# Attention with a compressive memory, mixed with a gated MLP: the memory update on four column groups, placed behind a visit's logits

## The chip, the cores and the metric

The kernel runs on one core of a Trainium2 chip. A core has a matrix engine (TensorE, "PE", with its weight loads shown apart as "PEld"), three engines for element-wise work (VectorE "DVE", ScalarE "ACT", GpSimd "POOL"), a queue for transfers (SyncE "SP"), and two memories: SBUF, 128 partitions, and PSUM, into which PE alone writes its products. The metric is the device time of one execution in microseconds, as the median of several runs. Profiles are of one more execution.

## What is computed

Cut from the reference; B = 1, S = 2048 tokens, D = 512, 32 heads of 16 channels, 4 segments of L = 512 tokens, MLP width 1792. All inputs are bf16.

```python
g = sigmoid((x * gate_w).sum(-1))                 # a gate for each token
return g * A(x) + (1 - g) * B(x)

def B(x):                                         # gated MLP
    return (gelu(x @ w_gate) * (x @ w_up)) @ w_down

def A(x):                                         # attention by segments, with a memory
    q, k, v = x @ wq, x @ wk, x @ wv              # as (head, segment, L, 16)
    phi = lambda t: where(t > 0, t + 1, exp(t))
    M, z = 0, 0                                   # for each head 16 x 16, and 16
    for s in range(4):
        p = softmax(qs @ ks.T * 16 ** -0.5 + causal_mask)
        a_dot = p @ vs
        a_mem = (phi(qs) @ M) / (phi(qs) @ z + 1e-6)
        o = sigmoid(beta) * a_mem + (1 - sigmoid(beta)) * a_dot
        M = M + phi(ks).T @ vs
        z = z + phi(ks).sum(over tokens)
    return concat(o) @ wo
```

The memory update of the last two lines of the loop is what the change is about. It is needed after segments 0, 1 and 2.

## The kernel before

Channels lie on partitions and tokens in the free dimension for q and k: four blocks `c` of 128 channels, which are eight heads each. Scores are computed transposed, 64 keys at a time, with the softmax left unnormalized (no row maximum; a bound on the logits that is computed on the way decides at the end whether a slow general branch has to redo the work, which these inputs don't need).

**Visits.** The work around the change is ordered by hand, when the program is built, by a loop over 72 *visits* (lines 991 to 1034), 18 for each segment (`NP`). A visit issues the logits of one or two key blocks (`group_qk`, line 643: matmuls of 32 rows by 128 columns of the array, the four heads of one parity in four row groups), one exponential over four PSUM banks on ACT, and causal selects on POOL. Two visits after the last block of a channel block follows its `lump`: 64 products of the probabilities with V (`pv`, line 663, arrays of 64 rows by 32 columns, tile `od`), their transposes on DVE (`oq`), normalization and transposes back over the next visits. `clock[0]` counts visits.

**Fill.** Between visits PE works on units from several streams: projections (`qT`, `kT`, `vT`, `zT`), the MLP (`gT`, `uT`, `dT`), the output product (`aT`), and the memory (`MT`, `zd`). Each unit is a tuple of a PE estimate, a DVE estimate and a generator; units have conditions and due times, and `fill_to` takes the most urgent one until the estimated time of the visit (`goal`) is reached. `left()` adds the PE estimates of all units that are still waiting, and the loop spreads the resulting slack over the remaining visits. A unit with an estimate of 0.0 is issued as soon as its condition holds (`heads`), and `later(n, f)` defers a step by n visits. All of this runs at build time; on the chip each engine runs its own instructions in the order of issue and waits on semaphores.

**PSUM.** Four banks hold the logits (`plg`), four single banks (`gen`) are taken in turn by everything else. `room_for_bank` lets a unit that is under way finish before too many banks are taken beside it.

**Memory.** After a segment's keys are done, phi(k) is formed in place in `ktb`, and four transposing DMAs on SP bring it to `pk` with tokens on partitions (`u_pk`, line 400). `u_M` (line 551) comes twice for a segment: it takes two channel blocks, and for each of them and each of four token blocks multiplies the 128 channels of phi(k) with the 8 heads of V and a column of ones (8 x 17 = 136 columns). Of the result only the diagonal blocks are wanted (a head's channels with the same head's V), but all eight heads' products for every channel are added into `Macc` (128 x 4 x 8 x 17, f32). `u_mask` (line 570) multiplies by the block mask `bm` to get the block-diagonal `Mn` (for the numerators, `mem_num`) and `Mz` (for the denominators, `u_den`). The units of stream "M" (line 881) are, for each segment, two of `u_M`, `u_mask`, two of `u_den`; `u_M` may start 3 visits after the last transposing DMA was issued (`pk_at`), and its due visit is 18 s + 10 (and + 12). The transposes of the next segment's phi(k) wait until both halves of the memory are counted (line 867).

Of the kernel before, what the change touches and what calls it, by code (L numbers as in the profile page):

```python
# [11 lines left out]
ALU = mybir.AluOpType  # L12

P = 128
D = 512
H = 32
DH = 16
NSEG = 4
# [35 lines left out]
def kernel(  # L54
# [43 lines left out]
    beta = const([P, H], BF, "beta")  # L98
    gh = const([P, H], F32, "gh")
    og = const([P, H], F32, "og")  # L100
    Macc = const([P, NC8, 8, 17], F32, "Macc")
    Mn = [const([P, NC8, 128], BF, f"Mn{i}") for i in range(2)]
    Mz = [const([P, NC8, 8], BF, f"Mz{i}") for i in range(2)]
    rdm = [const([P, KT, H], F32, f"rdm{i}") for i in range(2)]
# [443 lines left out]
            return MM512  # L548
        return 4 * MM512, EVAC, f

    def u_M(s, half):
        def f():
            T = gen("MT")
            Tv = T[:, 0:272].rearrange("p (c h e) -> p c h e", c=2, h=8)
            Tm = T[:, 0:272].rearrange("q (c j p e) -> q c j p e", c=2, j=4, p=2)
            for cc in range(2):
                c = 2 * half + cc
                for kt in range(KT):
                    nc.tensor.matmul(Tm[:, cc], lhsT=pk[:, kt, c * P:(c + 1) * P],  # L559
                                     rhs=Vh[s % 2][:, kt, :, 4 * c:4 * c + 4, 0:17]  # L560
                                     .rearrange("q p j e -> q j p e"),
                                     start=(kt == 0), stop=(kt == KT - 1))
                if cc == 0:
                    yield 0.3
            mv = Macc[:, 2 * half:2 * half + 2, :, :]
            nc.vector.tensor_tensor(out=mv, in0=mv, in1=Tv, op=ALU.add)
            return 0.3
        return 0.6, 0.4, f

    def u_mask(s):  # L570
        def half(h0):
            nc.vector.tensor_tensor(
                out=Mn[s % 2][:, h0:h0 + 2, :].rearrange("p c (h e) -> p c h e", h=8),
                in0=Macc[:, h0:h0 + 2, :, 0:16],
                in1=bm[:, None, :, 0:16].to_broadcast((P, 2, 8, 16)), op=ALU.mult)
            passed(0.0, 0.78)
            done["Mn", s] = count(("Mn", s)) + 1

        def f():
            if general_now[0]:  # L580
                half(0)
                half(2)
            nc.vector.tensor_tensor(out=Mz[s % 2][:, :, :], in0=Macc[:, :, :, 16],
                                    in1=bm[:, None, :, 16].to_broadcast((P, NC8, 8)),
                                    op=ALU.mult)
            if not general_now[0]:
                later(2, lambda: half(0))
                later(8, lambda: half(2))
        return 0.0, 0.2, f
# [274 lines left out]
    us = []  # L864
    for s in range(NSEG - 1):
        us += [unit(u_pk(s, c), 0, ("pk", s), lambda s=s, c=c: ("k", s, c - c % 2) in ready
                    and (s == 0 or count(("M", s - 1)) == 2)) for c in range(NC8)]
    streams.append(Stream("T", us))

    def u_x3():  # L870
# [9 lines left out]

    us = []
    for s in range(NSEG - 1):
        us += [unit(u_M(s, half), NP * s + 10 + 2 * half, ("M", s),
                    lambda s=s: count(("pk", s)) == NC8 and clock[0] >= pk_at[s] + 3)
               for half in range(2)]
        us.append(unit(u_mask(s + 1), 0))
        us += [unit(u_den(s + 1, pair), NP * s + 16 + 9 * pair, ("den", s + 1),
                    lambda s=s, pair=pair: ("q", s + 1, 2 * pair) in ready)
               for pair in range(2)]
# [101 lines left out]
    for pieces in visits:  # L991
        clock[0] += 1
        for i, b, off in pieces:
            s, c = i // NC8, i % NC8
            need(("k", s), c + 1)
            need(("q", s), c + 1)
            if i % NC8 == 0 and s not in oTs:
                oTs[s] = wk2.tile([P, FC, L], BF, name="oT", tag="oT")
        s = pieces[0][0] // NC8
        t = group_qk(pieces)  # L1000
        passed(QK_T)
        for i, b, off in pieces:
            blocks.setdefault(i, {})[b] = (t, off)
            if len(blocks[i]) == NB:
                lumps.append((clock[0] + 2, i))
        t_act[0] = max(t_act[0], t_pe[0] + TURN) + EXP_T
        act_left[0] -= EXP_T
        ready_at = t_act[0]
        if lumps and lumps[0][0] == clock[0]:
            i = lumps.pop(0)[1]  # L1010
            need(("v", i // NC8), KT + 1)
            heads()
            lump(i)
        for f in due.pop(clock[0], []):
            f()
        n = len(visits) - clock[0]
        pe_left = left() - TAIL_FILL - KT * 4 * MM512 + n * (QK_T + 0.22 * PV_T + 0.05)
        slack = t_pe[0] + pe_left - (t_act[0] + act_left[0] + n * (QK_T + TURN))
        goal = ready_at + max(0.0, slack) / (n + 1)
        if s == NSEG - 1:  # L1020
            goal = min(goal, t_pe[0] + 0.5 + left() - TAIL_FILL - KT * 4 * MM512)
        limit[0] = goal + QK_T + TURN + 0.1
        fill_to(t_pe[0] + 0.5 * (goal - t_pe[0]))
        for f in pending:
            f()
        pending.clear()
        fill_to(goal)
        t_pe[0] = max(t_pe[0], ready_at)
        limit[0] = 0.0
        for i in range(NC8, NSEG * NC8):  # L1030
            if last(i) - 1 == clock[0]:
                asked.append((i // NC8, i % NC8))
        if asked and can_num(*asked[0]):
            pending.append(lambda a=asked.pop(0): numerator(*a))
# [62 lines left out]
    def general():  # L1097
        general_now[0] = True
        queue[0] = nc.gpsimd
        nc.gpsimd.memset(Macc[:, :, :, :], 0.0)  # L1100
        nc.vector.tensor_copy(hm[:, :], bm[:, :, 16])
        for s in range(NSEG):
            oT = wk2.tile([P, FC, L], BF, name="oT", tag="oT")
            oTs[s] = oT
            if s % NX == 0:
                rows = G[(s + 1) % NG][:, 0:KT, :]
                nc.gpsimd.dma_start(rows, x2[s * L:(s + 1) * L, :]
                                    .rearrange("(k p) d -> p k d", p=P))
                for fc in range(FC):
                    turn(xS[s % NX][:, fc, :].rearrange("p (k t) -> p k t", k=KT),  # L1110
                         rows[:, :, fc * P:(fc + 1) * P])
            for c in range(NC8):
                run(u_k(s, c))
                run(u_q(s, c))
            for kt in range(KT):
                run(u_v(s, kt))
            run(u_vz(s))
            run(u_vs(s))
            if s > 0:
                for c in range(0, NC8, 2):  # L1120
                    phi_now(pq[:, c:c + 2, :], QT[:, c:c + 2, :])
                run(u_mask(s))
                run(u_den(s, 0))
                run(u_den(s, 1))
            neg = G[(s + 1) % NG][:, 8, 0:P]
            nc.gpsimd.memset(neg, 0.0)
            nc.gpsimd.affine_select(out=neg, in_=neg, pattern=[[-1, P]], compare_op=ALU.is_ge,
                                    fill=-1e9 * DH ** 0.5, base=0, channel_multiplier=1)
            for c in range(NC8):
                o2 = wk2.tile([P, 16, 2, DH], BF, name="o2", tag="o2")  # L1130
                if s > 0:
                    mem_num(s, c)
                tiles = {}
                for b in range(5):
                    t = ptp.tile([P, 4, 512], BF, name="pT", tag="pT")
                    tiles[b] = (t, 0)
                    if 1 <= b <= 3:
                        tiles[NB - b] = (t, L - 64 * b)
                general_blocks(s, c, tiles)
                oq = pv(s, c, tiles)  # L1140
                for p in range(2):
                    norm(c, p, oq[p], o2)
                back(c, o2, oT)
                if s > 0:
                    add_mem(s, c, oT)
            for hs in range(HS):
                run(u_gate(s, hs, False))
            gelu(s)
            for hs in range(HS):
                run(u_up(s, hs))  # L1150
            for qt in range(KT):
                run(u_down(s, qt))
            for qt in range(KT):
                run(u_out(s, qt))
            if s < NSEG - 1:
                for c in range(0, NC8, 2):
                    phi_now(ktb[:, c:c + 2, :], ktb[:, c:c + 2, :])
                for c in range(NC8):
                    run(u_pk(s, c))
                for half in range(2):  # L1160
                    run(u_M(s, half))

    flag = nc.alloc_registers("safe", engines=[mybir.EngineType.PE, mybir.EngineType.DVE,
                                               mybir.EngineType.Activation,
# [36 lines left out]
```

## Time and profile before

| | us |
|---|---|
| median of 3 runs (lowest, highest) | 269.65 (269.63, 270.01) |
| the profiled execution, its own time | 270.29 |
| its span, first to last instruction | 268.6 |
| `lg` products (line 649), 512, mean of one | 0.287 |
| exp of a visit on ACT (line 654), 72, mean of one | 1.876 |
| `MT` products (line 559), 48 of 128x136, mean of one | 0.227 |
| weight loads of `MT`, 48, mean of one | 0.097 |
| add into `Macc` (line 566), 6 of 128x272, median | 0.423 |
| mask into `Mn` (line 572), 6 of 128x256, median | 0.512 |
| mask into `Mz` (line 583), 3 of 128x32, median | 0.218 |
| transposing DMA to `pk` (line 406), 12, median from issue to landing | 2.5 |

The length of a PE instruction in a profile is that of a pipelined operation: many overlap, and their ends are modelled. What a product costs PE is therefore read from one start to the next. The shape behind an instruction, as in `128*128 128x136`, gives rows by columns of the array that the weights occupy, then partitions by elements of the output. "PEclk" or the number behind the busy times of a stretch is the granted clock of PE; it is 1.00 in every stretch of this run. The memory steps run at 57.6 and 63.2 us (segment 0), 119.3 and 127.6 (segment 1), 190.7 and 196.6 (segment 2).

### The profile page before, as it was taken

How to read it: one execution, taken by the hardware profiler on the slowest of the kernel's cores; microseconds unless marked ns; L12 is line 12 of the kernel's file. 1: busy time of each engine (PE TensorE's matmuls, PEld its weight loads, DVE VectorE, ACT ScalarE, POOL GpSimd, SP SyncE). 2: the span in 40 equal slices, each digit the busy share in tenths (PEclk: the TensorE clock that was granted, in tenths of full speed). 3: DMA queues.
4: the chain of work that ended last, by engine and by line, in shares of the span. 5: the costliest groups of instructions: out<-in, count | busy, mean ns of one | idle time of the engine just before them, and what ended most of it. 6: DMA issues, size and time to landing. Idle time of an engine off the chain costs nothing.

```text
span 268.6 us, 6586 instructions
## 1 busy us (share of the span) xinstructions
PE 263.5 (98%) x2717; PEld 118.8 (44%) x2717; DVE 203.9 (76%) x392; ACT 209.1 (78%) x163; POOL 156.8 (58%) x298
## 2 busy tenths in 40 slices
PE   7999999999999999999999999999999999999994
PEld 4454444444454444544444444444454544444442
DVE  2899575958778787697985979686889479698374
ACT  4226889999997998889999988889888987657510
POOL 4000158897914979986920998596785069655500
PEclk9999999999999999999999999999999999999999
DMA  7999901200070000300042001100000300002102
GB/s 217 322 202 326 340 13 39 42 4 0 9 156 2 0 21 23 78 4 20 2 61 76 10 21 42 42 20 22 20 23 21 67 2 20 2 20 42 40 22 83
DMA packets 30409, 16.59 MB, mean 62 GB/s; under 512 B 20008, under 2 KB 29096, under 8 KB 30376
## 3 DMA queue, kind: packets, MB, share of 16 engines
q1 hardware_dynamic: 30376, 16.14, 23.1%
q8 instruction: 22, 0.36, 0.6%
q14 instruction: 11, 0.09, 0.1%
HBM read 8.14 MB, written 2.10 MB: 38 GB/s over the span
## 4 chain that ended last, share of the span: by engine, by line
PE 88%; POOL 5%; issue 4%; DVE 1%; ACT 1%; ACTq 0%; DVEq 0%; POOLq 0%
PE gT L473 19%; PE uT L494 17%; PE dT L510 14%; PE lg L649 8%; PE od L674 6%; PE qT L290 5%; PE kT L376 5%; PE aT L532 5%; PE vT L414 4%; POOL pT L658 3%; POOL KTm L386 2%; PE MT L559 1%; PE warm L166 1%; PE mn L628 1%; ACT pT L654 1%
## 5 line engine op out<-in xcount | busy, mean ns | idle before, releaser
L658 POOL TENSOR_SCALAR_AFFINE_SELECT pT<-pT 64x256 bf16<-64x256 bf16 x256 | 113.9, 445 | 94.8 <-ACT pT L654 81.9
L654 ACT ACTIVATE pT<-lg 128x2048 bf16<-128x2048 f32 x72 | 135.1, 1876 | 24.9 <-PE lg L649 21.6
L494 PE MATMUL uT<-x,wup 128*128 128x512 bf16 x224 | 60.4, 380 | 0.0
L473 PE MATMUL gT<-x,wga 128*128 128x512 bf16 x224 | 57.0, 380 | 0.0
L510 PE MATMUL dT<-wdn,G 128*128 128x512 bf16 x224 | 52.9, 380 | 0.0
L500 DVE TENSOR_TENSOR G<-uT,G 128x512 bf16<-128x512 f32 x56 | 38.1, 683 | 6.4 <-PE uT L494 6.2
L386 POOL TENSOR_SCALAR KTm<-ktb,eo 128x512 bf16<-128x512 bf16 x26 | 40.6, 1572 | 1.3
L681 DVE STREAM_TRANSPOSE oq<-od 128x512 f32<-128x512 f32 x32 | 21.0, 695 | 19.3 <-PE od L674 19.3
L510 PEld LDWEIGHTS <-G 128*128 128x128 bf16 x224 | 20.8, 98 | 25.0 <-issue 2.1
L473 PEld LDWEIGHTS <-wga 128*128 128x128 bf16 x224 | 20.4, 98 | 23.9 <-issue 2.2
L494 PEld LDWEIGHTS <-wup 128*128 128x128 bf16 x224 | 19.8, 97 | 24.0 <-issue 5.4
L649 PE MATMUL lg<-QT,KTm 32*128 32x192 bf16 (+7 forms) x512 | 28.6, 287 | 0.0
L313 DVE CAST G<-gT 128x512 bf16<-128x512 f32 x24 | 16.5, 687 | 9.8 <-PE gT L473 9.6
L649 PEld LDWEIGHTS <-KTm 32*128 32x128 bf16 x512 | 8.3, 92 | 28.4 <-issue 28.0
L674 PE MATMUL od<-pT,V 64*32 64x128 bf16 (+7 forms) x512 | 19.4, 284 | 0.2 <-POOL pT L658 0.2
L674 PE MATMUL od<-pT,Vs 64*32 64x128 bf16 (+7 forms) x512 | 19.4, 284 | 0.0
L488 ACT ACTIVATE G<-G 128x3584 bf16<-128x3584 bf16 x6 | 18.8, 3182 | 0.0
L687 DVE SCALAR_TENSOR_TENSOR o<-oq,ogs,rden 128x256 bf16<-128x256 f32 x32 | 17.0, 532 | 1.1
L376 PE MATMUL kT<-x,wk 128*128 128x512 bf16 x64 | 17.2, 388 | 0.4 <-DVE x L189 0.4
L290 PE MATMUL qT<-x,wq 128*128 128x512 bf16 x64 | 16.6, 379 | 0.0
L532 PE MATMUL aT<-wo,oT 128*128 128x512 bf16 (+1 forms) x68 | 16.5, 367 | 0.0
L538 DVE SCALAR_TENSOR_TENSOR tB<-aT,gct,tB 128x512 bf16<-128x512 f32 (+1 forms) x17 | 12.0, 714 | 6.0 <-PE aT L532 5.7
(96 smaller groups left out, 277.2 us busy)
## 6 DMA issues: line engine op xcount, KB each, us to landing
wup<-in_B_w_up_dram SPq DMA_DIRECT2D x1, 1792.0 KB, 8.3
wdn<-in_B_w_down_dram SPq DMA_DIRECT2D x1, 1792.0 KB
out_dram<-tB SPq DMA_DIRECT2D x13, 128.0 KB, 1.7
wga<-in_B_w_gate_dram SPq DMA_DIRECT2D x1, 1280.0 KB, 10.6
Vs<-V SPq DMA_DIRECT2D x8, 144.0 KB, 2.6
G<-in_A_x_dram SPq DMA_DIRECT2D x2, 256.0 KB, 3.0
wk<-in_A_wk_dram SPq DMA_DIRECT2D x2, 256.0 KB, 4.3
wq<-in_A_wq_dram SPq DMA_DIRECT2D x1, 512.0 KB, 5.9
```

Source lines behind the costliest of these rows:

```text
L290: nc.tensor.matmul(T[:, :], lhsT=wq[:, fc, c * P:(c + 1) * P], rhs=xS[s % NX][:, fc, :], start=(fc == 0), stop=(fc == FC - 1))
L376: nc.tensor.matmul(T[:, :], lhsT=wk[:, fc, c * P:(c + 1) * P], rhs=xS[s % NX][:, fc, :], start=(fc == 0), stop=(fc == FC - 1))
L386: eng.tensor_scalar(out=KTm[:, (NC8 * s + c) % NK, :, p, :], in0=ktb[:, c, :].rearrange("q (b k) -> q b k", b=NB), scalar1=eo[:, p:p + 1], ...
L473: nc.tensor.matmul(T[:, :], lhsT=wga[:, fc, hs * P:(hs + 1) * P], rhs=xS[s % NX][:, fc, :], start=(fc == 0), stop=(fc == FC - 1))
L494: nc.tensor.matmul(T[:, :], lhsT=wup[:, fc, hs * P:(hs + 1) * P], rhs=xS[s % NX][:, fc, :], start=(fc == 0), stop=(fc == FC - 1))
L500: nc.vector.tensor_tensor(out=g, in0=T[:, :], in1=g, op=ALU.mult)
L510: nc.tensor.matmul(T[:, :], lhsT=G[s % NG][:, hs, qt * P:(qt + 1) * P], rhs=wdn[:, hs, :], start=(hs == 0), stop=(hs == HS - 1))
L532: nc.tensor.matmul(T[:, 0:w], lhsT=oT[:, fc, qt * P:(qt + 1) * P], rhs=wo[:, fc, d0:d0 + w], start=(fc == 0), stop=(fc == FC - 1))
L649: nc.tensor.matmul(lg[:, j, off:off + n], lhsT=KTm[rows, i % NK, b].rearrange("r p k -> r (p k)"), rhs=QT[rows, i % NC8, 64 * b:L], start= ...
L654: nc.scalar.activation(pT[:, :, :], lg[:, :, :], AF.Exp, scale=DH ** -0.5)
L658: nc.gpsimd.affine_select(out=v, in_=v, pattern=[[0, 4], [1, 64]], compare_op=ALU.is_ge, fill=0.0, base=0, channel_multiplier=-1)
L674: nc.tensor.matmul(od[p][32 * j:32 * j + 32, 64 * b:L], lhsT=w[:, 18 * h:18 * h + 32], rhs=t[rows, j, off:off + n], start=(b == 0), stop=( ...
```

## The change

`u_M` goes away. In its place `memory(s)` computes all four channel blocks at once, in one PSUM bank. Each channel block is cut into four groups of 32 channels, which are two heads each; a group's products run in its own 32 columns of the array (`tile_position=(0, 32 * j)`) against the 2 x 17 = 34 columns of its two heads' V. So it has 4 x 4 x 4 = 64 products of 128 rows by 32 columns and 34 elements where two `u_M` have 16 of 128 by 128 and 136. One add of 128 x 136 follows where there were two of 128 x 272.

`Macc` shrinks to 128 x 4 x 2 x 17: a partition keeps the two heads of its group of 32. `u_mask` broadcasts them over the four groups when it multiplies by `bm`, one channel block at a time, and forms `Mz` first.

`memory(s)` is no unit of a stream. It is issued in the visit loop, right behind a visit's logits and exp and ahead of a `lump` and of the fill, in the first visit that is at least 3 past the last `pk` transpose and at least 18 s + 10. The loop's estimate of PE time advances by 0.6 us; nothing of it is in `left()`. `u_mask` gets the condition that the memory is done.

```diff
-    Macc = const([P, NC8, 8, 17], F32, "Macc")
+    Macc = const([P, NC8, 2, 17], F32, "Macc")
...
-    def u_M(s, half):
...
-        return 0.6, 0.4, f
+    def memory(s):
+        T = gen("MT")
+        for c in range(NC8):
+            for kt in range(KT):
+                for j in range(4):
+                    nc.tensor.matmul(
+                        T[32 * j:32 * j + 32, 34 * c:34 * c + 34]
+                        .rearrange("q (p e) -> q p e", p=2),
+                        lhsT=pk[:, kt, P * c + 32 * j:P * c + 32 * j + 32],
+                        rhs=Vh[s % 2][:, kt, :, 4 * c + j, 0:17],
+                        start=(kt == 0), stop=(kt == KT - 1), tile_position=(0, 32 * j))
+        nc.vector.tensor_tensor(
+            out=Macc[:, :, :, :], in0=Macc[:, :, :, :],
+            in1=T[:, 0:34 * NC8].rearrange("q (c p e) -> q c p e", c=NC8, p=2), op=ALU.add)
+        done["M", s] = 1
 
     def u_mask(s):
         def half(h0):
+            for c in (h0, h0 + 1):
+                nc.vector.tensor_tensor(
+                    out=Mn[s % 2][:, c, :].rearrange("q (j p d) -> q j p d", j=4, p=2),
+                    in0=Macc[:, c, None, :, 0:16].to_broadcast((P, 4, 2, DH)),
+                    in1=bm[:, :, 0:16].rearrange("q (j p) d -> q j p d", j=4), op=ALU.mult)
+            passed(0.0, 0.6)
+            done["Mn", s] = count(("Mn", s)) + 1
+
+        def f():
             nc.vector.tensor_tensor(
...
+                out=Mz[s % 2][:, :, :].rearrange("q c (j p) -> q c j p", j=4),
+                in0=Macc[:, :, None, :, 16].to_broadcast((P, NC8, 4, 2)),
+                in1=bm[:, None, :, 16].to_broadcast((P, NC8, 8))
+                .rearrange("q c (j p) -> q c j p", j=4), op=ALU.mult)
...
-        us += [unit(u_M(s, half), NP * s + 10 + 2 * half, ("M", s),
-                    lambda s=s: count(("pk", s)) == NC8 and clock[0] >= pk_at[s] + 3)
-               for half in range(2)]
-        us.append(unit(u_mask(s + 1), 0))
+        us.append(unit(u_mask(s + 1), 0, None, lambda s=s: count(("M", s)) == 1))
...
         t = group_qk(pieces)
         passed(QK_T)
+        for z in range(NSEG - 1):
+            if (count(("M", z)) == 0 and count(("pk", z)) == NC8 and
+                    clock[0] >= max(pk_at[z] + 3, NP * z + 10)):
+                room_for_bank()
+                memory(z)
+                passed(0.6, 0.3)
```

The condition of line 867 becomes `count(("M", s - 1)) == 1`, and the general branch calls `memory(s)`.

More of the change, by code (lines that the diff above doesn't have):

```diff
@@ L549, in u_out @@
         return 4 * MM512, EVAC, f
-    def u_M(s, half):
[L552 to L567, printed above, removed]
-        return 0.6, 0.4, f
+    def memory(s):
[13 more added lines that the diff above has]
+        done["M", s] = 1
@@ L570, in u_mask @@
     def u_mask(s):
         def half(h0):
[L572 to L576, printed above, removed]
+            for c in (h0, h0 + 1):
[3 more added lines that the diff above has]
+                    in1=bm[:, :, 0:16].rearrange("q (j p) d -> q j p d", j=4), op=ALU.mult)
@@ L577, in half @@
+            passed(0.0, 0.6)
             done["Mn", s] = count(("Mn", s)) + 1
         def f():
+            nc.vector.tensor_tensor(
+                out=Mz[s % 2][:, :, :].rearrange("q c (j p) -> q c j p", j=4),
+                in0=Macc[:, :, None, :, 16].to_broadcast((P, NC8, 4, 2)),
+                in1=bm[:, None, :, 16].to_broadcast((P, NC8, 8))
+                .rearrange("q c (j p) -> q c j p", j=4), op=ALU.mult)
             if general_now[0]:
@@ L582, in f @@
                 half(2)
[L583 to L586, printed above, removed]
+            else:
                 later(2, lambda: half(0))
@@ L866 @@
         us += [unit(u_pk(s, c), 0, ("pk", s), lambda s=s, c=c: ("k", s, c - c % 2) in ready
-                    and (s == 0 or count(("M", s - 1)) == 2)) for c in range(NC8)]
+                    and (s == 0 or count(("M", s - 1)) == 1)) for c in range(NC8)]
     streams.append(Stream("T", us))
@@ L1159, in general @@
                     run(u_pk(s, c))
-                for half in range(2):
-                    run(u_M(s, half))
+                memory(s)
     flag = nc.alloc_registers("safe", engines=[mybir.EngineType.PE, mybir.EngineType.DVE,
```

## Prediction

> **What bounds the kernel now.** I read the page's busy shares and slices first, then the chain of waits, then busy time in five stretches, then single instructions of the stages that the change touches.
>
> ```profile
> PE 263.5 (98%) x2717; PEld 118.8 (44%) x2717; DVE 203.9 (76%) x392; ACT 209.1 (78%) x163; POOL 156.8 (58%) x298
> PE   7999999999999999999999999999999999999994
> PE 88%; POOL 5%; issue 4%; DVE 1%; ACT 1%; ACTq 0%; DVEq 0%; POOLq 0%
> 30.00:90.00 60.00, 60.00 (x647) 26.50 (x645) 44.78 (x86) 54.81 (x41) 40.24 (x72) 1.00 0.21 48
> 90.00:150.00 60.00, 59.99 (x664) 27.15 (x661) 49.58 (x96) 54.23 (x41) 41.80 (x78) 1.00 0.15 33
> 150.00:210.00 60.00, 60.00 (x669) 26.99 (x669) 47.89 (x92) 52.76 (x41) 45.47 (x84) 1.00 0.09 24
> ```
>
> The first two lines are the page's parts 1 and 2, the third its part 4, the rest a table by stretch (PE, PEld, DVE, ACT, POOL busy, then granted clock, 1.00 throughout). From 30 to 210 us PE has no hole. A busy PE may still hide switches and slow issue, so I went to its starts:
>
> ```profile
> 57.52 0.19 PE L674 MATMUL od<-pT,V 64*32 64x64 bf16 x1
> 57.64 0.68 PE L559 MATMUL MT<-V,pk 128*128 128x136 bf16 x8
> 58.16 0.59 PE L494 MATMUL uT<-x,wup 128*128 128x512 bf16 x2
> 58.69 0.40 PE L649 MATMUL lg<-QT,KTm 32*128 32x384 bf16 x8
> 59.02 0.60 PE L494 MATMUL uT<-x,wup 128*128 128x512 bf16 x2
> 59.46 1.03 PE L473 MATMUL gT<-x,wga 128*128 128x512 bf16 x4
> 60.32 0.92 PE L414 MATMUL vT<-wv,x 128*128 128x448 bf16 x4
> ```
>
> Columns: start, length of the merged group, instruction. Four gT of 512 columns take 60.32 - 59.46 = 0.86 us, so a column costs 0.42 ns. The two uT at 58.16 are streamed by 58.16 + 0.43 = 58.59, yet the logits, in another shape of the array (32 rows), start at 58.69: 0.10 us for the **change of shape**. The last od (64 columns, 0.03 us) ends at 57.55 and MT starts at 57.64: 0.09 again. I take 0.095 us for each change. PE thus waits for practically nobody; its total of streaming and switching is the time, with a start and a tail that the change does not touch.
>
> **What is removed.** Eight MT products hold PE from 57.64 to 58.16. The same line in the other five halves of the three memory steps, by stretches cut at the next instruction's start, gives 0.52, 0.53, 0.51, 0.52 and 0.51: 3.11 us in all, 1.04 per segment. Their 136 columns stream in 57 ns, their pace is 64. They stood among full-array fill, so they cost no change of shape.
>
> **What is added on PE.** Per segment 64 loads of 128 rows by 32 columns and 64 products of 34 columns, in 16 rounds of four column groups. No 128-by-32 shape is in the trace, so the price is bounded. From below by streaming:
>
> ```profile
> 75.56 0.65 PE L430 MATMUL zT<-wv,x 128*128 128x65 bf16 x16
> 76.05 0.34 PE L599 MATMUL zd<-Mz,pq 128*128 128x8 bf16 x8
> 76.25 0.38 PE L473 MATMUL gT<-x,wga 128*128 128x512 bf16 x1
> 57.47 0.09 PEld L674 LDWEIGHTS <-Vs 64*32 64x32 bf16 x1
> 57.48 0.09 PEld L674 LDWEIGHTS <-V 64*32 64x32 bf16 x1
> 57.48 0.09 PEld L674 LDWEIGHTS <-Vs 64*32 64x32 bf16 x1
> 57.49 0.09 PEld L674 LDWEIGHTS <-V 64*32 64x32 bf16 x1
> ```
>
> zT: 0.49 / 16 = 30 ns for 65 columns, of which 27 stream, so 3 ns come on top; 34 columns then take 14 + 3 = 17 ns, and 16 rounds with all loads hidden 0.28 us. From above: zd has 8 columns and still needs 0.20 / 8 = 25 ns for each load and product. If every one of the 64 pays that, 1.6 us. Between them lies PV, the row that resembles the new stage most (column groups of 32, a load for each product): its eight products of a round start 3 to 4 ns apart, and where its rounds get short, in the last four rows above, one load follows another by about 8 ns. At 8.3 ns a pair, 64 pairs take **0.53 us**. I take that: it is nearest in shape, and the bound by streaming lies under it.
>
> The Trainium skill speaks against it: "TensorEngine Tiling (Array Packing)", section Restrictions, says that column tiling gives up the fast weight load, and "TensorE: Matmul & The Clock Gate", section on LDWEIGHTS, gives a load its columns divided by 1.2 in ns. An estimate by those is 32 / 1.2 = 27 ns a load and 1.7 us a segment if the four groups' loads queue behind each other. PV's loads, which are column-tiled too, follow at 3 to 8 ns, so the trace does not bear out the queueing for 64 rows; for 128 rows no run here shows it.
>
> **Its place.** Behind the logits the array goes 32*128, 128*32, then fill or PV: one change of shape more than before, 0.095 us. Per segment 0.53 + 0.095 - 1.04 = -0.42, for three segments **-1.25 us**. Other ends of the same sum: streaming alone 3 x (0.28 + 0.095 - 1.04) = -2.0; zd's pace 3 x (1.6 + 0.095 - 1.04) = +2.0.
>
> **What I cost at nothing.** DVE: before, per segment two adds of 0.42, two masks of 0.52 and Mz of 0.28, 2.2 us; after, one add of half the size, four masks of half the size and Mz. Between Mz's 0.22 (32 elements) and the mask's 0.51 (256), a mask of 128 elements takes some 0.35, so 0.3 + 1.4 + 0.3 = 2.0; at the old sizes 0.42 + 4 x 0.52 + 0.41 = 2.9. Either way under 1 us a segment on an engine with a quarter of its time free and 1% of the chain. If that cover went, its lateness would reach PE through the four banks. The add now stands in DVE's queue right behind the logits, ahead of the evacuation of the unit that the visit interrupted and, in a visit with PV, of the oq transposes; it waits for MT, about 0.6 us, and DVE already sits idle 0.82 us for od in that same visit at 57 us. The stage issues no DMA and passes none on SP or POOL; its operand pk is issued at 51.15 us and landed at 53.68, while the earliest place is the logits at 56.21 (visit 11, where the old MT was as well). Behind the memory on PE stand PV or fill and then the next logits; a PV behind it comes 0.6 us later, but PV has its inputs for two visits. In the third segment the place moves from visit 54 (190.7 us) to about visit 49, as nothing but the landed pk holds it. Clearing Macc on POOL (0.55 us at 3.2) shrinks at a time when POOL is nearly idle.
>
> **Rivals.** (B) The four column groups' loads exclude each other. PV's loads alternate between two row halves; with all 128 rows in use the 8.3 ns becomes 16.6, and 64 of them 1.06 us: 3 x (1.06 + 0.095 - 1.04) = +0.35, **270.0 us**. For it: every column group shares all row groups. Against: PV's rounds stream at full pace for all but the last.
>
> (C) The slower side by price: each pair pays the 25 ns of zd, +2.0, **271.6 us**. For it: the only short products with 128-row loads in the trace do pay it. Against: zd has one group, so nothing can overlap it.
>
> (D) The slower side by the plan. The code places fill by its own estimates; the memory units (six of 0.6 us, 3.6) drop out of its count of work left, so up to 3.6 / 72 = 0.05 us less fill is set between visits and all later units can change order. Exp to logits has little room:
>
> ```profile
> 56.66 1.88 ACT L654 ACTIVATE pT<-lg 128x2048 bf16<-128x2048 f32 x1 [0.23 <-PE lg L649]
> ACT pT L654 <- PE lg L649: 21.6, 43, 1.4
> POOL pT L658 <- ACT pT L654: 81.9, 34, 28.7
> ```
>
> The exp ends at 58.54, the next logits start at 58.69; PE would wait if it came 0.15 us sooner. What such a wait costs is seen once: PV from 228.55 us waits for POOL's selects and takes 1.97 instead of 0.98. Two more such waits bring +2.0 - 1.25 = +0.75, **270.4 us**; from 1.25 us of waits the gain is gone, from 1.8 it is a loss. For it: the balance is close, PE waits only about 1 us in 235 now. Against: 43 of 72 exps wait for PE, so it is ACT that has the room (0.5 us each).
>
> (E) PE finishes its fill sooner but ends no sooner, **269.65 us**. Against it: the last exp ends at 251.8 us, and behind that PE alone works for 13 us.
>
> **How the numbers follow.** The sum is made on the profiled execution: span 268.6, its own time 270.29, so 267.35 and 269.05 after; its time is 0.64 above the median of the runs, 269.65, and the same difference on the median gives **268.4 us**. Chances: forecast 0.50 (267.6 to 268.9 by the streaming bound and a load pace up to 11 ns), B 0.17, C 0.10, D 0.15, E 0.08. The range of 267.6 to 271.0 holds the forecast, B, E and most of D; C and a small part of the other tails are left out. 0.2%, about what a measurement here can tell, is 0.54 us. Faster by more: nearly all of the forecast, a little of D and E, 0.52. Within: the rest of E, two thirds of B, a third of D, 0.24. Slower: C, the rest of B and D, 0.24.
>
> **What would show it.** Right: one MT stage per segment that holds PE for 0.3 to 0.7 us from its first start to the next instruction's, 0.09 us holes on both sides, two of them in visits 11 and about 29 to 30, no idle in PE between 30 and 228 us, and a span near 267.3. Starts of products 3 to 5 ns apart within a round of four and rounds at 17 to 33 ns bear out the overlap; an even spacing of 16 or 25 ns is B or C. New holes ahead of lg or od with POOL or ACT as releaser are D. The forecast fails if a stage takes over 0.95 us, where the sum is nil.

## The result and the profile after

The changed kernel runs in 268.50 us (median of 6 runs, 268.28 to 268.55) against 269.98 for the kernel before (6 runs, 269.63 to 270.46). The ratio is 0.9944 with a 95% interval of 0.9934 to 0.9954: 0.56% or 1.48 us less. Forecast were 268.4 us and a range of 267.6 to 271.0. The saving forecast was 1.25 us; the two times lie as near as they do also because the kernel before came out 0.33 us higher here than in the three runs that the forecast started from. The profiled execution took 268.51 with a span of 266.8, 1.8 us less than the profiled one of before.

From the page of the changed kernel (busy shares, then the chain by engine) and from its table by stretch (PE, PEld, DVE, ACT, POOL busy, granted clock, DMA):

```profile
PE 261.9 (98%) x2861; PEld 117.1 (44%) x2861; DVE 200.7 (75%) x394; ACT 209.7 (79%) x164; POOL 155.7 (58%) x298
PE 94%; DVE 4%; issue 1%; DVEq 0%
30.00:90.00 60.00, 60.00 (x697) 26.13 (x695) 44.59 (x87) 55.00 (x42) 39.77 (x72) 1.00 0.25 62
90.00:150.00 60.00, 59.93 (x714) 26.77 (x712) 50.21 (x98) 54.91 (x41) 41.59 (x78) 1.00 0.14 33
150.00:210.00 60.00, 60.00 (x722) 26.80 (x721) 45.33 (x93) 54.06 (x43) 43.85 (x80) 1.00 0.11 24
```

PE is as full as before, has 144 more instructions, and is 94% of the chain where it was 88%. It still sets the time, with less to do. The first memory stage in order of time, PE and DVE rows of the timeline of the changed kernel:

```profile
55.74 0.40 PE L649 MATMUL lg<-QT,KTm 32*128 32x448 bf16 x8
56.06 0.57 PEld L556 LDWEIGHTS <-pk 128*32 128x32 bf16 x64 [0.21 <-issue]
56.07 0.67 PE L556 MATMUL MT<-V,pk 128*32 128x34 bf16 x64
56.66 0.39 PE L494 MATMUL uT<-x,wup 128*128 128x512 bf16 x1
56.82 0.29 DVE L562 TENSOR_TENSOR Macc<-Macc,MT 128x136 f32<-128x136 f32 x1 [1.80 <-PE MT L556]
56.98 0.39 PE L674 MATMUL od<-pT,V 64*32 64x512 bf16 x1
```

The stage holds PE from 56.07 to 56.66, 0.60 us; the other two hold it 0.62 (112.4 us) and 0.60 (172.2). Between the stage and PV (`od`) stands one product of `uT`, an array shape of its own: that is the unit that the visit interrupted, which `room_for_bank` finished because memory and PV together take three banks.

**Where the time came from.** To compare whole traces I went through all starts on PE from the first logits to the end of the last product, counted what lies between stages of different array shape as change of shape, and put the rest to the tile that was being made:

| us | before | changed | difference |
|---|---|---|---|
| up to the first logits | 28.46 | 28.21 | -0.25 |
| MT | 3.07 | 1.51 | -1.56 |
| changes of shape (number) | 15.48 (160) | 16.15 (165) | +0.67 |
| PV (`od`), its waits included | 17.38 | 16.92 | -0.46 |
| `gT`, with the hole behind it | 36.54 | 36.35 | -0.19 |
| all other products | 164.03 | 164.05 | +0.02 |
| last product to the end of the span | 3.60 | 3.59 | -0.01 |
| span | 268.56 | 266.77 | -1.79 |

Only the second row is the change itself. The first row has nothing to do with the edit, as the last section shows. The PV row has two places: the PV at 137 us takes 0.22 us more (1.45 instead of 1.23), and that of visit 65 takes 0.69 less (1.30 instead of 1.99; most of the others take 1.01). Visit 65, by the kernel before and then by the changed one:

```profile
229.56 0.55 PE L674 MATMUL od<-pT,Vs 64*32 64x256 bf16 x2
230.34 0.24 PE L674 MATMUL od<-pT,V 64*32 64x192 bf16 x1 [0.24 <-POOL pT L658]
```

```profile
227.98 0.33 PE L674 MATMUL od<-pT,Vs 64*32 64x256 bf16 x2
228.34 0.24 PE L674 MATMUL od<-pT,V 64*32 64x192 bf16 x1
```

From the last products of one key block to the first of the next 0.78 us passed before, with POOL's select named as the releaser, and 0.36 after. The memory has no part in that visit; the fill around it stands in another order.

### The profile page after: what moved, and what is told of

Same layout as the page of the kernel before. It is cut to its first block, busy times and chain, and to the rows that moved or that the text cites. A ratio compares the mean times of both kernels' runs of the same rounds, so it can differ in the third digit from the quotient of the medians.

```text
span 266.8 us, 6876 instructions
## 1 busy us (share of the span) xinstructions
PE 261.9 (98%) x2861; PEld 117.1 (44%) x2861; DVE 200.7 (75%) x394; ACT 209.7 (79%) x164; POOL 155.7 (58%) x298
## 4 chain that ended last, share of the span: by engine, by line
PE 94%; DVE 4%; issue 1%; DVEq 0%
PE dT L510 19%; PE uT L494 18%; PE gT L473 18%; PE lg L649 8%; PE od L674 7%; PE kT L376 5%; PE qT L290 5%; PE aT L532 5%; PE vT L414 4%; PE mn L628 1%; PE warm L166 1%; PE zT L430 1%; DVE G L500 1%; PE MT L556 1%; PE x0T L183 1%
## 5 line engine op out<-in xcount | busy, mean ns | idle before, releaser
L473 PE MATMUL gT<-x,wga 128*128 128x512 bf16 x224 | 55.6, 380 | 0.0
L510 PE MATMUL dT<-wdn,G 128*128 128x512 bf16 x224 | 53.9, 380 | 0.0
L649 PE MATMUL lg<-QT,KTm 32*128 32x192 bf16 (+7 forms) x512 | 28.6, 287 | 0.0
L313 DVE CAST G<-gT 128x512 bf16<-128x512 f32 x25 | 17.1, 686 | 5.8 <-PE gT L473 5.6
L290 PE MATMUL qT<-x,wq 128*128 128x512 bf16 x64 | 16.6, 379 | 0.0
```

Of the source, the lines that this page charges most:

```text
L290: nc.tensor.matmul(T[:, :], lhsT=wq[:, fc, c * P:(c + 1) * P], rhs=xS[s % NX][:, fc, :], start=(fc == 0), stop=(fc == FC - 1))
L473: nc.tensor.matmul(T[:, :], lhsT=wga[:, fc, hs * P:(hs + 1) * P], rhs=xS[s % NX][:, fc, :], start=(fc == 0), stop=(fc == FC - 1))
L510: nc.tensor.matmul(T[:, :], lhsT=G[s % NG][:, hs, qt * P:(qt + 1) * P], rhs=wdn[:, hs, :], start=(hs == 0), stop=(hs == HS - 1))
L649: nc.tensor.matmul(lg[:, j, off:off + n], lhsT=KTm[rows, i % NK, b].rearrange("r p k -> r (p k)"), rhs=QT[rows, i % NC8, 64 * b:L], start= ...
```

## The experiments

The runs were made in three groups, each on another chip, with the kernel before in every group (medians 269.96, 269.99 and 269.92 us) and the changed kernel in the first and the last (268.30 in both). Twice the products, halves, the quarter and group by group are the second group, without the changed kernel beside them; where they are said to lie above or below it, the other groups' runs of it are meant. The number behind a time is the ratio to the kernel before with its 95% interval; it is not the quotient of the two medians (for the quarter 0.9882 against 0.9907), so tenths of a microsecond are read from medians and traces. "From first logits to the last product" leaves out the start, which differs between executions of one kernel.

**The changed kernel again.** No edit.

> The changed kernel once more, for comparison on the same chip: 0.994 of the kernel before, about 268.5 us, with three MT stages that hold PE for about 0.60 us each.

Measured: 268.30 us (5 runs), 0.9934 (0.9922 to 0.9947); once more beside the last group of runs 268.30 and 0.9941 (0.9924 to 0.9958). From first logits to the last product 234.96 us, before 236.50.

**The old shape in the new place.**

```diff
-        for c in range(NC8):
-            for kt in range(KT):
-                for j in range(4):
...
+        for half in range(2):
+            T = gen("MT")
...
+                    nc.tensor.matmul(Tm[:, cc], lhsT=pk[:, kt, c * P:(c + 1) * P],
+                                     rhs=Vh[s % 2][:, kt, :, 4 * c:4 * c + 4, 0:17]
+                                     .rearrange("q p j e -> q j p e"),
...
```

`Macc`, the adds and the masks are those of the kernel before; the place is that of the changed kernel. In the traces PE, DVE, ACT and POOL do all other work in the order of the changed kernel, but for a few products inside one PV.

> The plan of the changed kernel on every engine, but the memory's products in the old shape: 16 of 128x136 on the whole array, two adds of 128x272, masks of 128x256. Theory (the new shape's shorter hold of PE is the gain): MT streams 3.07 us instead of 1.51, and three changes of shape at 0.095 us drop out, so the time is 1.28 us above the changed kernel, about 269.8 us or 0.999 of before. Rival (the other order of the fill that the new plan happens to give is the gain): it stays at 268.5 us, 0.994.

Measured: 269.36 us (11 runs), 0.9979 (0.9970 to 0.9988); 1.06 above the changed kernel. In its trace MT takes 3.10 us instead of 1.51, three changes of shape are gone (162, 0.35 us), and so is a wait in the PV at 137 us, 0.30, which the expectation had not: 0.94 us more from first logits to the last product, 1.24 without that wait.

```profile
56.09 0.40 PE L646 MATMUL lg<-QT,KTm 32*128 32x448 bf16 x8
56.42 1.20 PE L559 MATMUL MT<-V,pk 128*128 128x136 bf16 x16
57.46 0.38 PE L494 MATMUL uT<-x,wup 128*128 128x512 bf16 x1
```

The same place as above, with 1.04 us from MT to uT instead of 0.60. So the shape is worth 1.06 us, and 0.6 us of the total gain come with the new place and order alone. Both theories were half right.

**The new shape among the fill.**

```diff
+    def u_M(s):
...
+            memory(s)
...
+        us.append(unit(u_M(s), NP * s + 10, ("M", s),
+                       lambda s=s: count(("pk", s)) == NC8 and clock[0] >= pk_at[s] + 3))
...
-        for z in range(NSEG - 1):
...
-                memory(z)
...
```

> The new shape as one unit among the fill, due where the old one was, counted in the work left with 0.6 us. Theory: each stage costs two changes of shape instead of one, so 3 x (0.50 + 0.19 - 1.02) = -1.0 us against before, about 269.0 us or 0.996, give or take 0.7 us for another order of the fill. Rival (the place behind the logits makes the gain): no gain, 1.000.

Measured: 268.10 us, 0.9930 (0.9917 to 0.9943). The rival falls: the place behind the logits is not needed. It did better than forecast, because this order has 164 changes of shape, where I had counted six more than the 160 of before, and its PV stages wait less (16.52 us).

**Twice the products.**

```diff
-        for c in range(NC8):
+        for c in list(range(NC8)) * (1 if general_now[0] else 2):
```

(`general_now[0]` is true only in the general branch, which these inputs don't need.)

> The memory's 64 products are issued twice into the same bank, the second time starting the sums anew; order and everything else as in the changed kernel. In the changed kernel the first 32 loads and products go in rounds of 25 ns, the last 32 evenly at 8.3 ns a pair. Theory (behind the first 32 pairs, which stand in PE's queue already, PE gets a pair only every 8.3 ns): all 96 further pairs at 8.3 ns, a stage holds 0.53 us longer, the time is 1.6 us above the changed kernel, about 270.1 us. Rival (the slower pace belongs to the last two channel blocks' operands): pairs 65 to 96 go in rounds of 25 ns again, 0.47 us longer a stage, 1.4 us in all.

Measured: 270.08 us (10 runs), 0.9985 (0.9962 to 1.0008); 1.6 to 1.8 us above the changed kernel's medians, and from first logits to the last product 236.57 against 234.96, 1.61 more. The times alone don't separate theory (1.6) from rival (1.4); the starts do.

```profile
55.87 1.20 PE L556 MATMUL MT<-V,pk 128*32 128x34 bf16 x128
57.00 0.39 PE L494 MATMUL uT<-x,wup 128*128 128x512 bf16 x1
```

128 pairs hold PE for 1.13 us, 64 for 0.60: 0.53 / 64 = 8.3 ns for each further pair. Start by start, the first eight rounds of four begin about 25 ns apart, and from pair 33 to 128 one pair follows another by 8.3 ns; a 31 ns gap in one of the three stages is the only exception. The blocks that were slow the first time stay slow, and those that were fast become slow: the operands are not it.

**In halves.**

```diff
-    def memory(s):
+    def memory(s, part=(0, 1, 2, 3)):
...
-        for c in range(NC8):
+        for c in part:
...
-                memory(z)
-                passed(0.6, 0.3)
+                k = 2 * count(("M", z))
+                memory(z, (k, k + 1))
+                passed(0.3, 0.2)
```

> Two channel blocks (32 pairs) behind the logits of one visit, the other two behind those of the next, each with its own add of 128x68. Theory (PE's queue holds the first 32 pairs, the rest come at 8.3 ns): every half goes in 8 rounds of 25 ns, 0.20 us, with no even stretch of 8.3 ns; 0.3 us less streaming in six stages, 0.3 us or more of added changes of shape, so the time is within 0.7 us of the changed kernel. Rival (blocks 2 and 3 are slow by their operands): the second half runs at 8.3 ns a pair, 0.27 us.

Measured: 268.91 us (10 runs), 0.9952 (0.9928 to 0.9976). The halves are in neighbouring visits:

```profile
55.87 0.38 PE L558 MATMUL MT<-V,pk 128*32 128x34 bf16 x32
56.17 0.39 PE L494 MATMUL uT<-x,wup 128*128 128x512 bf16 x1
...
58.68 0.38 PE L558 MATMUL MT<-V,pk 128*32 128x34 bf16 x32
58.99 0.39 PE L494 MATMUL uT<-x,wup 128*128 128x512 bf16 x1
```

Each of the six halves holds PE for 0.31 to 0.32 us, change of shape included, the second as fast as the first, and none has a stretch of 8.3 ns. MT takes 1.29 instead of 1.51 us, three more changes of shape take 0.22 of it back, and from first logits to the last product it is 234.95 us, as in the changed kernel. The median is 0.4 to 0.6 us longer all the same. In the trace 0.4 us of that lie behind the last product: 3.97 us to the end of the span instead of 3.59. DVE's last evacuation of full width starts 0.14 us ahead of the last product there, and 0.51 us ahead in the changed kernel; the fill stands in another order, here at the end too.

**A quarter of the products.**

```diff
-            for kt in range(KT):
+            for kt in range(KT if general_now[0] else 1):
...
-                        start=(kt == 0), stop=(kt == KT - 1), tile_position=(0, 32 * j))
+                        start=(kt == 0), stop=(kt == KT - 1 or not general_now[0]), tile_position=(0, 32 * j))
```

> Only the first of the four token blocks enters the memory's products, 16 pairs instead of 64; the memory leaves out three quarters of each segment's tokens. Theory (PE's time is the kernel's time, one to one): a stage streams 0.10 instead of 0.50 us, the time is 1.2 us below the changed kernel, about 267.3 us. Rival (what PE saves turns into waiting for ACT or POOL): it stays within 0.3 us of 268.5.

Measured: 267.48 us (4 runs), 0.9882 (0.9833 to 0.9932), 0.8 to 1.0 below the changed kernel. MT falls from 1.51 to 0.34, the wait of PV on POOL grows by 0.2, and from first logits to the last product it is 234.96 - 233.98 = 0.98 less: what PE saves, the kernel saves, less a fifth that becomes a wait.

**Group by group.**

```diff
-            for kt in range(KT):
-                for j in range(4):
+            for j in range(4):
+                for kt in range(KT):
```

> The same 64 products, but a column group's four token blocks follow each other, then the next group's, so that neighbours in time share a column group. Theory (a round of 25 ns is one group's load, then its product, and four groups overlap): without neighbours to overlap with, each pair costs 25 ns but for one in four, a stage about 1.3 to 1.6 us, the time 2.4 to 3.3 us above the changed kernel, 270.9 to 271.8 us. Rival (only the supply of instructions counts, and loads overlap whatever the group): no change, 268.5 us.

Measured: 268.59 us (10 runs), 0.9942 (0.9921 to 0.9963); 0.3 above the changed kernel.

```profile
55.86 0.77 PE L556 MATMUL MT<-V,pk 128*32 128x34 bf16 x64
56.55 0.39 PE L494 MATMUL uT<-x,wup 128*128 128x512 bf16 x1
```

The stage holds PE 0.70 us instead of 0.60, far from 1.3. My theory falls. In the trace the first four products, which share a group, start at 0, 14, 27 and 39 ns, and from there on two starts fall into each such step, though the order of issue has one group after the other: 32 pairs take 0.22 us, nearly as short as in the changed kernel (0.20). So a group needs no 25 ns for its next load, and neighbours overlap without being written side by side. Behind the 34th pair the starts become uneven, up to 33 ns apart, and the last 30 pairs take 0.345 us, 11.5 ns each instead of 8.3; there lies most of what the stage loses. What sets the 25 ns of a round, and this second pace, is open.

**Two groups of 64 channels.**

```diff
-                for j in range(4):
+                for j in range(2):
                     nc.tensor.matmul(
-                        T[32 * j:32 * j + 32, 34 * c:34 * c + 34]
+                        T[64 * j:64 * j + 64, 68 * c:68 * c + 68]
...
-                        start=(kt == 0), stop=(kt == KT - 1), tile_position=(0, 32 * j))
+                        start=(kt == 0), stop=(kt == KT - 1), tile_position=(0, 64 * j))
...
```

`Macc` and the masks keep four heads for each channel instead of two.

> The plan of the changed kernel, but two column groups of 64 channels with 68 columns each: 32 pairs a stage instead of 64, twice the streaming. Theory (behind 32 queued pairs the pace is set by the supply of pairs, 8.3 ns each, not by streaming): 16 rounds of 28 + 3 ns make 0.50 us, as long as the 64 finer pairs take, so the time equals that of the changed kernel within 0.1%. Rival (the streamed columns set the stage, or a load of 64 columns is slower): a stage of 0.8 us or more, 0.9 us above the changed kernel.

Measured: 268.68 us (6 runs), 0.9946 (0.9928 to 0.9964), beside 0.9941 for the changed kernel; from first logits to the last product 235.02 against 234.92. Rounds of two go every 32 ns, streaming, to the end:

```profile
56.21 0.71 PE L556 MATMUL MT<-V,pk 128*64 128x68 bf16 x32
56.85 0.39 PE L494 MATMUL uT<-x,wup 128*128 128x512 bf16 x1
```

0.64 us a stage against 0.60. Halving the streamed columns a second time, from 68 to 34, is worth next to nothing (0.04 us a stage): what 34 columns save is lost in the second half of the 64 pairs, at 8.3 ns a pair.

**The new shape in the old order.** Line by line the order of the kernel before on every engine; in each of its six memory units 32 pairs of the new shape.

```diff
-                for kt in range(KT):
-                    nc.tensor.matmul(Tm[:, cc], lhsT=pk[:, kt, c * P:(c + 1) * P],
...
+                for kt in range(KT):
+                    for j in range(4):
+                        nc.tensor.matmul(
+                            T[32 * j:32 * j + 32, 34 * cc:34 * cc + 34]
...
```

`Macc` and the masks are those of the changed kernel.

> The plan of the kernel before on every engine, in which each of the six memory units holds 32 pairs of the new shape instead of 8 products of 128x136. Theory (shape alone): six stages of 0.21 us for 3.07 us, and nine more changes of shape (two for each stage, less three that stand beside logits or PV anyway) at 0.095 us, so 1.29 + 0.86 - 3.07 = -0.9 us against before, 0.9966, about 269.05 us. Rival (only the new order of the fill gains): 1.000 of before.

Measured: 270.11 us (12 runs), 1.0013 (0.9998 to 1.0027). No gain, as the rival had it, though not for the rival's reason: in the trace MT falls by 1.75 us to 1.32, nine more changes of shape cost 1.04, and waits in the fill grow, so that 0.46 us are left at the last product (236.04 against 236.50). In this execution the tail then takes 4.05 instead of 3.60 us; DVE's first instruction behind the branch that ends the kernel came 1.1 us after it, before 0.5. Whether the tail does so in every execution can't be seen from one trace, so that half is open. What the run shows is that, cut into six stages, the changes of shape and the waits take back three quarters of what the new shape saves.

```profile
62.13 0.81 PE L473 MATMUL gT<-x,wga 128*128 128x512 bf16 x3
62.87 0.38 PE L558 MATMUL MT<-V,pk 128*32 128x34 bf16 x32
63.19 0.39 PE L494 MATMUL uT<-x,wup 128*128 128x512 bf16 x1
```

Three `gT` are streamed by 62.13 + 0.65 = 62.78, and MT starts at 62.87; its last product, of 14 ns, starts at 63.07, uT at 63.19. Two holes of 0.1 us for a stage of 0.2.

**Away from PV.** The loop waits for a visit without PV:

```diff
-                    clock[0] >= max(pk_at[z] + 3, NP * z + 10)):
+                    clock[0] >= max(pk_at[z] + 3, NP * z + 10) and
+                    not (lumps and lumps[0][0] == clock[0])):
```

> The changed kernel, but the memory waits for a visit without the PV products. In the changed kernel a visit with PV goes logits, MT, the interrupted uT, od, fill: four changes of shape where before there were two. Theory: two visits save one change each, 0.19 us in all, so 268.3 us or 0.9993 of the changed kernel; the order of the fill changes too and may move it by up to 0.7 us either way. Rival (a PV beside the stage costs nothing): no difference beyond that of the order.

Measured: 267.92 us (6 runs), 0.9930 (0.9915 to 0.9944). And a second time, beside the changed kernel:

> The memory in the first visit without PV, once more beside the changed kernel: two changes of shape less and the waits of PV on POOL at 137 and 228 us gone, against a new one of 0.17 us at 194, 0.3 to 0.45 us below it, 0.9985.

Measured: 268.12 us (6 runs), 0.9930 (0.9912 to 0.9947), the changed kernel 268.30. By the timed runs the two can't be told apart with certainty. In both traces it has 163 changes of shape instead of 165, and 234.58 and 234.59 us from first logits to the last product against 234.92 to 234.97 in three traces of the changed kernel: 0.36 us less, half of it (0.18) changes of shape, the rest PV waits (16.67 against 16.89).

## Why the prediction was right, step by step

**PE as the bound.** Right up to the last product: the quarter takes 1.17 us from PE and is 0.98 us shorter there. The time need not follow in full: halves and the new shape in the old order lose 0.4 us behind the last product.

**The stage at 0.53 us.** Measured 0.50 (1.51 / 3) without changes of shape. The row it was taken from is a few loads of PV's last round, 8.3 ns one behind another; the products of that round start 3 to 4 ns apart, so it was no price of a pair of load and product. The second half of a stage runs at the same number, 0.28 us for 32 pairs; the first half is faster, 0.20 us. So the value was right by a mixture that I had not foreseen, and in part by luck. Rivals B and C, 16.6 or 25 ns for every pair, didn't come: 25 ns is what four pairs take. The rule of the Trainium skill that weighed against the change was that of no fast weight load with column tiling ("TensorEngine Tiling (Array Packing)", section Restrictions), and by "TensorE: Matmul & The Clock Gate", LDWEIGHTS, an estimate of some 27 ns a load. It does no harm here: a round's four loads start 2 to 4 ns apart and four pairs take 25 ns together.

The pace changes behind 32 pairs, which are 64 instructions. That agrees with the queue depth of 64 that the opening table of "TensorE: Matmul & The Clock Gate" in the Trainium skill gives for TensorE. That the queue is the cause is a reading of two runs (twice the products, halves), not shown by itself. A change after a time instead of a number of pairs is not excluded, though in group by group, where the 32nd pair comes a little later (0.22 us behind the first instead of 0.20), the change comes later too. And why PV's last loads stand 8.3 ns apart, although its rounds of eight pairs before them take 0.06 to 0.22 us and leave time to fill a queue, is open.

**"one change of shape more than before".** This step failed in part: three were expected, 0.29 us, and there are five. Of the 0.67 us in the table they are 0.5; the other 0.15 are two logits that start 0.07 us late (at 109.5 and 123.0 us), which belongs to the order of the fill (old shape in new place has them too). In two of the three visits (11 and 29) PV follows, and the interrupted `uT` is finished between the stage and PV, so logits, MT, uT, PV, fill make four changes where there were two. I had named the visits and named PV as the next in the queue, but had not followed the count in `room_for_bank`. Old shape in new place has exactly these two (162 instead of 160), so they come with the place and the other three with the shape; waiting for a visit without PV takes the two back.

**The other order of the fill (D).** I had it as a loss of 0.75 us with a chance of 0.15. It came with the other sign: the PV at 229 us waits 0.69 us less, the 0.18 us hole at 133 us went, the PV at 137 us waits 0.22 us more, and two logits come late. The first of these, with the exp before it, in the changed kernel:

```profile
107.58 1.88 ACT L654 ACTIVATE pT<-lg 128x2048 bf16<-128x2048 f32 x1 [0.25 <-PE lg L649]
109.50 0.40 PE L649 MATMUL lg<-QT,KTm 32*128 32x512 bf16 x4
```

The exp ends at 109.46 and the logits, which go into the banks that it reads, start 0.04 us behind it: the new wait on ACT that D foresaw, only 0.07 us long and twice. Old shape in new place measures order and place together, the two changes of shape included: -0.6 us. Without it the change would have given 0.9 to 1.1 us instead of 1.5 to 1.7. Rival E, a gain that turns into waiting, did not come.

**The sum.** Forecast -1.25; by the trace -1.56 (MT) + 0.67 (shapes) - 0.65 (order) - 0.25 (start) = -1.79 for this pair of executions, -1.48 by the medians. The three stages were priced at 1.59 us and took 1.51; what went was counted as 3.11 and was 3.07. Two errors of 0.4 and 0.65 us stood against each other, so that the total is better than its parts; that is luck.

**Costed at nothing.** Right. DVE's add took 0.296 us, a mask 0.282 (median), Mz 0.216, together 1.64 a segment where 2.0 were expected; DVE idled 3.7 us for MT in three places, and PE waited for none of it. The stages are in visits 11, 29 and 48, as expected (11, 29 or 30, about 49).

## What to carry to other kernels

Where PE is full, cutting useless columns pays, but price the stage with its loads and its changes of shape: here 64 small pairs took 0.50 us where their columns stream in 0.23, five changes of shape took back 0.5 of 1.56 us, and six stages in the old order left nothing that could be measured. Before an insertion behind or ahead of a stage, follow what the bank or buffer accounting will squeeze in between. And when an order is computed from estimates, run the old work in the new order once: only that tells the edit's worth from the order's.

## What was unexpected of the hardware

- Small column-tiled pairs of load and product whose column groups take turns run in rounds of 25 ns for four up to the 32nd pair of a stage, then at 8.3 ns each for as long as the stage lasts (96 pairs in the longest). That a product of 34 columns and one of 68 fill a stage of nearly the same length (0.60 and 0.64 us) follows from it.
- The load for a column group mostly starts 1 to 2 ns after another group's product has started, over the same 128 rows. "TensorE: Matmul & The Clock Gate", Part 3, of the Trainium skill lets a load overlap a running product only in other row groups (or into the background weights). These stages don't agree with the rule; whether the words in brackets are the reason, no run here shows.
- The start up to the first logits took 27.9 to 28.6 us in most profiled executions and 30.0 in one, which took 270.39 us, where all other runs of the same kernel took 268.2 to 268.8. The first projections of K, in that execution and in another of the same kernel, up to 8 us:

```profile
6.38 1.89 PE L376 MATMUL kT<-x,wk 128*128 128x512 bf16 x4 [0.72 <-DMA wk<-in_A_wk_dram]
6.12 2.12 PE L376 MATMUL kT<-x,wk 128*128 128x512 bf16 x9 [0.93 <-DMA wk<-in_A_wk_dram]
```

  The first of them follows its weights in both, and starts 0.26 us later in the slower execution. The rest of the difference is not the weights: no later load there waits for a DMA, yet the products start 427 ns apart up to 9.77 us and 216 ns apart from 10.02 on, while in the other they are 216 ns apart from the second on. The trace's record of the granted clock begins (with 1.00) at 9.82 us in the slower one and at 4.54 in the other; the 1.00 that a table by stretch gives for 6.3 to 9.8 us there hides this. In the pair of the result the record begins at 7.04 us before and at 6.51 after, and the first three steps from one K product to the next take 1.11 us before and 0.86 after, which is the 0.25 us of the table's first row. So two profiles can differ by the moment from which PE runs at full pace, without any edit behind it.
